# Fewer weight pieces under way beside the feed-forward layers, and half a weight tile requested earlier

## The chip, the cores and the metric

The kernel runs on one core of one Trainium2 chip. A core has a matrix engine (TensorE, PE in the profile), a vector engine (VectorE, DVE), a scalar engine (ScalarE, ACT), a general engine (GpSimd, POOL) and a queue engine (SyncE, SP) that here mainly issues transfers between the chip's memory and the core's own memory. Sixteen DMA engines carry these transfers. The metric is the time of one execution in microseconds (us), as the median of several runs.

## The reference

The program joins two layers. An attention layer with 8 batches, 8 heads, 576 positions and 64 numbers a head (causal in blocks of 64) gives 4608 tokens of 512 numbers. A layer of 8 experts then sends each token to one expert by a gate; an expert keeps at most its 80 best tokens, and every other token's output is zero:

```python
scores = np.where(block_i >= block_j, scale * q @ k.T, -1e9)
attn = softmax(scores);  x = (attn @ v) as (4608, 512)
expert_idx = argmax(x @ w_gate);  gate_w = softmax(x @ w_gate)[expert_idx]
for e in range(8):
    tok_idx = the 80 tokens of expert e with the largest gate_w
    h = np.maximum(x[tok_idx] @ w1[e], 0.0)          # w1[e]: 512 x 1024
    out[tok_idx] = gate_w[tok_idx, None] * (h @ w2[e])  # w2[e]: 1024 x 512
```

All numbers are float32, so an expert's two matrices are 2 MB each and the sixteen of them 32 MB.

## The kernel before, in words

**Attention** takes the first three quarters of the time. It goes over 32 pairs of heads by a table written out by hand, and writes the tokens to a scratch tensor `xs` in the chip's memory (`store_x`, line 391, issued by POOL).

**Selection** follows: the gate's values are ranked, and the numbers of each expert's 80 tokens come out as `gi` (line 1037). POOL then gathers the tokens of the first three experts from `xs` by indirect transfers (`fetch`, line 1027); the first gather needs all writes of `xs` and `gi`.

**The feed-forward layers** start when the first gather has landed. PE turns the tokens (`prepare`, line 1157) and multiplies weights as the stationary operand with 80 tokens as the moving one (`blocks`, line 1144). The order on PE is layer 1 of expert 0, layer 1 of expert 1, layer 2 of expert 0, and so on to layer 2 of expert 7, which is cut in two: three of its four output blocks first, then the last one.

**Weights.** `weights` (line 313) allocates a 2 MB tile and requests it in four pieces (`PARTS`) of 512 KB. The list of 16 tiles (line 309) is in the order of use. The first four go out early through POOL (`early`). The other twelve, 48 pieces, go out through SP's queue at line 327; this text numbers these pieces 1 to 48. Pieces 1 to 8 are two tiles that take memory of the closing attention layer, pieces 9 to 20 three more (`fwa`, `fwc`, `fwb`), and pieces 21 to 48 take the place of tiles that PE has used up; they are asked for in the loop over the experts (lines 1218 and 1224).

SP takes its instructions in order, and what it waits for is set at line 328: a piece waits until the piece three before it (`UNDERWAY`) has landed, so that at most three are under way. Pieces 9 to 20 wait besides for the second gather (`fetches[HOLD]`, line 1124), which the first of them holds back for all behind it. A piece into a used tile waits for PE too.

Of the kernel before, what the change touches and what calls it, by code (L numbers as in the profile page):

```python
# [19 lines left out]
BLK = 64  # L20
NT = 5
FW0, FWA, FWC, FWB = 4, 3, 1, 1
PARTS, UNDERWAY = 4, 3
KPOOL = 2
FIRST, BEHIND = 3, 28
LATER = {(1, 0, 0): 1, (1, 0, 1): 1, (1, 1, 0): 1, (1, 1, 1): 1, (2, 0, 0): 1}
# [129 lines left out]
def tile_attn_moe(ctx, tc, q, k, v, w_gate, w1, w2, capacity, out, xs=None, dbg=None):  # L156
# [3 lines left out]
    E, _, F = w1.shape  # L160
# [88 lines left out]
    before = const.tile([P, P], F32, name="before")  # L249
    after = const.tile([P, P], F32, name="after")  # L250
# [55 lines left out]
    nw = 0  # L306
    wpools = [wp] * FW0

    wlist = [(w1, 0)] + [x for e in range(E) for x in ((w1, e + 1), (w2, e))][0:-2] + [(w2, E - 1)]
    wt_ = {}  # L310
    parts_ = []

    def weights(n, after=None, parts=PARTS, underway=UNDERWAY):

        nonlocal nw
        for _ in range(n):
            src, e = wlist[nw]
            w_ = wpools[nw % len(wpools)].tile([P, KP * F], F32, name="w")
            nw += 1
            wt_[src is w2, e] = w_ = w_.rearrange("p (a f) -> p a f", f=src.shape[2])  # L320
            if nw <= FW0:
                early_.append((w_, src[e].rearrange("(a p) f -> p a f", p=P)))
                continue
            view = src[e].rearrange("(a p) f -> p a f", p=P)
            na = w_.shape[1]
            for a in range(0, na, na // parts):
                load = nc.sync.dma_start(w_[:, a:a + na // parts], view[:, a:a + na // parts]).ins
                for before in ((after,) if after is not None else ()) + tuple(parts_[-underway:][:1] if len(parts_) >= underway else ()):
                    tc.add_manual_dep(load, before.name, mybir.DependencyInfo(
                        mybir.DependencyClass.Sync, mybir.DependencyReason.DATA))  # L330
                parts_.append(load)
# [6 lines left out]
    def early(n):  # L338

        nonlocal begun  # L340
        while n:
            if begun % PARTS == 0:
                weights(1)
            w_, view = early_[-1]
            na = w_.shape[1]
            m = min(n, PARTS - begun % PARTS) if n >= PARTS else 1
            a = slice(na * (begun % PARTS) // PARTS, na * (begun % PARTS + m) // PARTS)
            nc.gpsimd.dma_start(w_[:, a], view[:, a])
            begun += m
            n -= m  # L350
# [462 lines left out]
    n = B * NP  # L813
# [96 lines left out]
    with tc.issue_after(batches[B - 1].stored.ins):  # L910
        pool.indirect_dma_start(
            out=trial, out_offset=None, in_=q.rearrange("b h s d -> (b h s) d"),
            in_offset=bass.IndirectOffsetOnAxis(ap=none.bitcast(U32), axis=0),
            bounds_check=NTOK - 1, oob_is_err=False)
    weights(2)
    sel2 = late.enter_context(tc.tile_pool(name="sel2", bufs=1, **right, **tw))

# [42 lines left out]
    HOLD = 1  # L960
# [65 lines left out]
    def fetch(e, after=None):  # L1026
        load = pool.indirect_dma_start(
            out=xg[e], out_offset=None, in_=xs[:, :],
            in_offset=bass.IndirectOffsetOnAxis(ap=gi[:, e:e + 1].bitcast(U32), axis=0),
            bounds_check=NTOK - 1, oob_is_err=False).ins  # L1030
        if after is not None:
            tc.add_manual_dep(load, after.ins.name, mybir.DependencyInfo(
                mybir.DependencyClass.Sync, mybir.DependencyReason.DATA))
        return load
# [3 lines left out]
    fetches = [fetch(e) for e in range(min(FIRST, E))]  # L1038
# [13 lines left out]
    def finish(after):  # L1052

        with tc.issue_after(after.ins), tc.issue_after(fetches[FIRST - 1]):
            finish_()
# [65 lines left out]
    fwc = late.enter_context(tc.tile_pool(name="fwc", bufs=FWC, **right, **tw))  # L1121
    fwb = late.enter_context(tc.tile_pool(name="fwb", bufs=FWB, **tw))
    wpools += [fwc] * FWC + [fwb] * FWB
    weights(FWA - 2 + FWC + FWB, fetches[HOLD])

    def divide(dst, src, a0=0, a1=NP):

# [38 lines left out]
    def first(e, x_, between=None):  # L1166
        hT = fx.tile([P, FP, CHUNK], F32, name="hT", bufs=3)
        w_ = wt_[False, e]
        for f in range(2):
            ph = ps_s.tile([P, 512], F32, name="ps")  # L1170
            for n_, mm in enumerate(blocks(lambda b: ph[:, b * CHUNK:(b + 1) * CHUNK],
                                           w_[:, :, 512 * f:512 * (f + 1)], x_, KP, 4)):
                if n_ == BEHIND:
                    more(1, e, f, mm)
            nc.scalar.activation(hT[:, 4 * f:4 * (f + 1)].rearrange("p a s -> p (a s)"), ph[:, 0:4 * CHUNK], AF.Relu)  # L1175
            if f == 0 and between is not None:
                between(mm)
        return hT

    def second(e, hT):  # L1180
        py = ps_a.tile([P, 512], F32, name="av")
        for n_, mm in enumerate(blocks(lambda b: py[:, b * CHUNK:(b + 1) * CHUNK], wt_[True, e], hT, FP, KP)):
            if n_ == BEHIND:
                more(2, e, 0, mm)
        yT = fx.tile([P, KP, CHUNK], F32, name="yT", bufs=2)
        vec.tensor_copy(yT.rearrange("p a s -> p (a s)"), py[:, 0:KP * CHUNK])  # L1186
        return yT

    def scatter(e, yT, cuts=(0, KP)):
        y = fx.tile([CHUNK, DM], F32, name="y", bufs=3)  # L1190
        for a0, a1 in zip(cuts, cuts[1:]):
            tp = ps_m.tile([P, 512], F32, name="pm")
            for a in range(a0, a1):
                turned = nc.tensor.transpose(tp[0:CHUNK, a * P:(a + 1) * P], yT[:, a], ident)  # L1194
            vec.tensor_scalar(y[:, a0 * P:a1 * P], tp[0:CHUNK, a0 * P:a1 * P], scalar1=comb[:, 1, e:e + 1], scalar2=None,  # L1195
                              op0=ALU.mult)
            if a1 < KP:
                yield turned
        pool.indirect_dma_start(  # L1199
            out=out[:, :], out_offset=bass.IndirectOffsetOnAxis(ap=si.bitcast(U32)[:, e:e + 1], axis=0),  # L1200
            in_=y, in_offset=None, bounds_check=NTOK - 1, oob_is_err=False)
# [5 lines left out]
    def ready(x, after=None):  # L1207
        xs_[x], divided[x] = prepare(x, after)

    ready(0)  # L1210
    for e in range(E):
        if e + 1 < E and e > 0:
            ready(e + 1)
        if e >= 2:
            for _ in scatter(e - 2, yT_[e - 2]):
                pass
        hT_[e] = first(e, xs_[e], (lambda mm: ready(1, mm)) if e == 0 else None)
        weights(int(nw < len(wlist)))
        if e >= 1:
            yT_[e - 1] = second(e - 1, hT_[e - 1])  # L1220
        if e == 1:
            finish(divided[2])
        if e >= 1:
            weights(int(nw < len(wlist)))
    yl = fx.tile([P, KP, CHUNK], F32, name="yT", bufs=2)
    CUTS = (0, KP - 1, KP)
    tail = scatter(E - 1, yl, CUTS)
# [217 lines left out]
```

## Time and profile before

| what | us |
|---|---|
| median of 3 runs (lowest, highest) | 400.22 (397.24, 400.84) |
| the profiled execution's own time | 396.4 |
| its span, first to last instruction | 394.6 |
| PE busy | 376.5 (95%) |
| DVE busy | 279.9 (71%) |
| ACT busy | 265.1 (67%) |
| POOL busy | 254.7 (65%) |
| TensorE clock granted, of full speed | 0.997 |
| share of PE in the chain that ended last | 82% |

Times in the views count from the first instruction. The profiled execution is one run: the 1.8 us between its span and its time lie before the first and behind the last instruction. The median of the timed runs is 3.8 us above it. A busy PE is not PE at its peak. In the chain of waits, a piece named "issue" is time in which the engine waited for nothing that the profile shows.

### The profile page before, as it was taken

Reading aid. Unit: us, or ns where it says so; the run is one execution under the profiler, and the core shown is the slowest. Engines: PE = TensorE matmul, PEld = TensorE weight load, DVE = VectorE, ACT = ScalarE, POOL = GpSimd, SP = SyncE. Lnnn points to the kernel's source line nnn. Section 1 sums busy time; section 2 is a strip of 40 time slices with the busy share of each in tenths; the row PEclk is TensorE's granted clock in tenths of the full one; section 3 lists DMA queues with packets and bytes.
Section 4 is the critical chain, followed back from the end, with each engine's and each line's share of the span. In section 5 each row is a group of like instructions: output and inputs, shape, how many; then the busy total and the mean of one; then the engine's idle time right before and its main releaser. Section 6 shows DMA issues by size and latency. Waiting matters only on the chain.

```text
span 394.6 us, 15556 instructions
## 1 busy us (share of the span) xinstructions
PE 376.5 (95%) x6351; PEld 292.2 (74%) x6351; DVE 279.9 (71%) x646; ACT 265.1 (67%) x702; POOL 254.7 (65%) x439
## 2 busy tenths in 40 slices
PE   8898999999999999999999999999987989999992
PEld 4576777777777777777777777767765979999892
DVE  5877989998998999899899989988673131111111
ACT  2799898999998999999899989999431111111000
POOL 7889977897798789789979887822567400000011
PEclk9999999999999999999999999999999999999998
DMA  9999999979897898999999999999374999999911
GB/s 139 149 155 152 151 156 197 223 149 226 202 186 167 183 214 201 219 245 257 189 225 271 212 211 240 287 293 312 83 257 132 307 293 321 328 309 305 318 57 39
DMA packets 120125, 84.43 MB, mean 214 GB/s; under 512 B 94446, under 2 KB 96494, under 8 KB 120049
## 3 DMA queue, kind: packets, MB, share of 16 engines
q1 hardware_dynamic: 102432, 45.55, 51.5%
q0 software_dynamic: 15808, 37.52, 40.7%
q8 instruction: 52, 0.85, 1.0%
q10 hardware_dynamic: 1808, 0.31, 0.4%
q14 instruction: 25, 0.20, 0.2%
HBM read 63.22 MB, written 20.33 MB: 212 GB/s over the span
## 4 chain that ended last, share of the span: by engine, by line
PE 82%; POOL 7%; DMA 5%; issue 2%; DVE 2%; POOLq 0%; DVEq 0%
PE sc L650 23%; PE sc L786 20%; PE ps L1144 11%; PE sc L737 11%; PE av L1144 8%; POOL ld L582 2%; PE sc L408 2%; DMA xs<-Y 2%; DMA vn<-in_v_dram 2%; PE sc L745 2%; PE sc L427 1%; PE pm L1194 1%; POOL xs L391 1%; POOL vn L595 1%; PE pm L1157 1%
## 5 line engine op out<-in xcount | busy, mean ns | idle before, releaser
L707 ACT ACTIVATE P<-sc,negm 128x448 f32<-128x448 f32 (+3 forms) x256 | 146.0, 584 | 10.5 <-DVE negm L686 4.1
L686 DVE TENSOR_REDUCE negm<-sc 128x1 f32<-128x448 f32 (+4 forms) x224 | 127.1, 616 | 10.8 <-PE sc L657 9.2
L650 PE MATMUL sc<-T,T 64*128 64x64 f32 (+4 forms) x768 | 111.7, 414 | 2.8 <-POOL T L631 2.1
L650 PEld LDWEIGHTS sc<-T,T 64*128 64x128 f32 x768 | 71.1, 187 | 34.2 <-issue 24.3
L582 POOL DMA_DIRECT2D ld<-in_k_dram x120 | 81.8, 693 | 1.6 <-DMA vn<-in_v_dram 1.0
L798 ACT COPY PT<-sc 128x1024 f32<-128x1024 f32 x63 | 60.8, 1016 | 12.5 <-PE sc L737 11.6
L786 PE MATMUL sc<-PT,vn 128*64 128x128 f32 (+1 forms) x512 | 60.8, 379 | 0.6 <-ACT PT L798 0.6
L737 PE MATMUL sc<-ident,P 64*128 64x64 f32 x1280 | 53.8, 227 | 0.1
L707 ACT ACTIVATION_READ_ACCUMULATOR P<-sc,negm 128x1 f32 x256 | 53.0, 207 | 0.0
L786 PEld LDWEIGHTS sc<-PT,vn 128*64 128x64 f32 x512 | 33.8, 137 | 23.4 <-issue 22.2
L1199 POOL DMA_INDIRECT out_dram<-y,si x8 | 7.4, 924 | 66.7 <-DVE y L1195 60.5
L737 PEld LDWEIGHTS sc<-ident,P 64*128 64x128 f32 x1280 | 45.2, 139 | 3.2 <-ACT P L707 1.2
L628 DVE STREAM_TRANSPOSE T<-ld 128x576 f32<-128x576 f32 x62 | 47.3, 764 | 0.0
L1144 PE MATMUL ps<-xsT,w 128*64 128x80 f32 x1024 | 40.3, 234 | 1.5 <-issue 1.5
L595 POOL DMA_DIRECT2D vn<-in_v_dram x64 | 39.7, 626 | 2.1 <-DMA vn<-in_v_dram 1.6
L1144 PEld LDWEIGHTS ps<-xsT,w 128*64 128x64 f32 x1024 | 37.4, 137 | 3.7 <-issue 2.9
L631 POOL TENSOR_SCALAR T<-T 128x576 f32<-128x576 f32 x31 | 20.7, 668 | 28.6 <-DVE negm L686 13.9
L1186 DVE COPY yT<-av 128x320 f32<-128x320 f32 x7 | 3.4, 492 | 47.5 <-PE av L1144 47.5
L1175 ACT ACTIVATE hT<-ps 128x320 f32<-128x320 f32 x16 | 7.0, 438 | 42.4 <-PE ps L1144 34.4
L1144 PE MATMUL av<-hT,w 128*64 128x80 f32 x896 | 32.9, 233 | 0.7 <-issue 0.7
L1144 PEld LDWEIGHTS av<-hT,w 128*64 128x64 f32 x896 | 32.1, 137 | 0.8 <-issue 0.8
L800 DVE COPY xT<-sc 128x576 f32<-128x576 f32 x31 | 23.3, 752 | 11.5 <-PE sc L764 11.5
(193 smaller groups left out, 526.5 us busy)
## 6 DMA issues: line engine op xcount, KB each, us to landing
w<-in_moe_w_dram SPq DMA_DIRECT2D x48, 512.0 KB
out_dram<-zero SPq DMA_DIRECT2D x18, 512.0 KB
ld<-in_q_dram SPq DMA_DIRECT2D x124, 72.0 KB
ld<-in_k_dram POOLq DMA_DIRECT2D x120, 72.0 KB, 4.9
xs<-Y POOLq DMA_DIRECT2D x28, 288.0 KB, 5.7
vn<-in_v_dram POOLq DMA_DIRECT2D x32, 128.0 KB, 6.3
vn<-in_v_dram POOLq DMA_DIRECT2D x64, 64.0 KB, 5.4
w<-in_moe_w_dram POOLq DMA_DIRECT2D x8, 512.0 KB, 7.0
```

The costliest lines, as they stand in the source:

```text
L582: eng.dma_start(self.nat[x][r], (q, k)[x][self.b, self.h0 + h, :, 32 * i:32 * i + 32] .rearrange("(g r) d -> r g d", r=32))
L595: nc.gpsimd.dma_start(self.vn[c * BLK:(c + 1) * BLK, 1], turned[:, :, 1 - c])
L628: nc.vector.transpose(t, self.nat[x].rearrange("p g d -> p (g d)"))
L631: nc.gpsimd.tensor_scalar(t, t, scalar1=SCALE, scalar2=1.0, op0=ALU.mult, op1=ALU.mult)
L650: nc.tensor.matmul(to[h], lhsT=self.T[0][r, q:q + P], rhs=self.T[1][r, k0:k1], start=start, stop=stop)
L686: nc.vector.tensor_reduce(to, src, axis=AX.X, op=ALU.max, negate=True)
L707: nc.scalar.activation(dst, src, AF.Exp, bias=self.negm[0:n, u, h:h + 1], scale=1.0, accum_out=self.bt.sums[0:n, u, self.h0 + h:self.h0 + ...
L737: nc.tensor.transpose(pt[:, c, to(c, n_)], row[u][r, h, k(u, h, j):k(u, h, j) + P], ident[r, r])
L786: nc.tensor.matmul(to, lhsT=lhs, rhs=rhs, start=(n_ == 0), stop=(n_ == len(steps) - 1))
L798: nc.scalar.copy(*self.out.pop((what, x)))
L800: nc.vector.tensor_copy(*self.out.pop((what, x)))
L1144: yield nc.tensor.matmul(dst(b)[64 * c:64 * (c + 1)], lhsT=w_[:, a, col:col + 64], rhs=x_[:, a], start=(a == 0 and b == 0), stop=(a == n - ...
```

## The change

`weights` gets a parameter `free`: the first `free` pieces of the first tile of a call do not wait for what `after` names. The call for pieces 9 to 20 has `free=2`, so pieces 9 and 10 no longer wait for the second gather. And the calls in the loop over the experts (pieces 21 to 48) use `LATE`, 2, in place of `UNDERWAY`, 3: such a piece waits for the piece two before it.

```diff
-PARTS, UNDERWAY = 4, 3
+PARTS, UNDERWAY, LATE = 4, 3, 2
...
-    def weights(n, after=None, parts=PARTS, underway=UNDERWAY):
+    def weights(n, after=None, parts=PARTS, underway=UNDERWAY, free=0):
...
-        for _ in range(n):
+        for i in range(n):
...
-                for before in ((after,) if after is not None else ()) + tuple(parts_[-underway:][:1] if len(parts_) >= underway else ()):
+                for before in ((after,) if after is not None and (i or a >= free * na // parts) else ()) + tuple(parts_[-underway:][:1] if len(parts_) >= underway else ()):
...
-    weights(FWA - 2 + FWC + FWB, fetches[HOLD])
+    weights(FWA - 2 + FWC + FWB, fetches[HOLD], free=2)
...
-        weights(int(nw < len(wlist)))
+        weights(int(nw < len(wlist)), underway=LATE)
...
-            weights(int(nw < len(wlist)))
+            weights(int(nw < len(wlist)), underway=LATE)
```

The instructions of PE, DVE, ACT and POOL and their order stay as they are; so does the order of SP's transfers. Only waits of SP differ. In the rows below, a transfer waits for counters: `DMAHW0` to `DMAHW7` belong to transfers of SP's queue, which take them in turn, `DMASW0` to `DMASW7` to POOL's in the same way. The gather that is waited for is on `DMASW0`; earlier transfers of POOL are on it too.

SP's queue, pieces 9 to 14 of the change (piece 9 is on `DMAHW3`, so piece 12 waits for it):

```order
L327 DMA w<-in_moe_w_dram 128x2x512 [waits DMASW5_49,DMASW4_49,DMASW6_49,DMASW3_49,DMASW7_49,DMASW1_49,DMAHW0_49,DMASW0_49,Activation_49]
L327 DMA w<-in_moe_w_dram 128x2x512 [waits DMAHW1_49]
L327 DMA w<-in_moe_w_dram 128x2x512 [waits DMAHW2_49,DMASW0_49]
L327 DMA w<-in_moe_w_dram 128x2x512 [waits DMAHW3_49]
L327 DMA w<-in_moe_w_dram 128x1024 [waits DVE_49,PE_49,DMAHW4_49,Activation_49,Pool_49]
L327 DMA w<-in_moe_w_dram 128x1024 [waits DMAHW5_49]
```

The wait for the gather is new on piece 11. Piece 9 waits for `DMASW0` in both kernels, in the change only for the transfers of the attention layer that used its memory.

SP's queue, pieces 21 to 26 before (piece 21 is on `DMAHW7`):

```order
L327 DMA w<-in_moe_w_dram 128x1024 [waits DMAHW4_49,PE_49]
L327 DMA w<-in_moe_w_dram 128x1024 [waits DMAHW5_49]
L327 DMA w<-in_moe_w_dram 128x1024 [waits DMAHW6_49]
L327 DMA w<-in_moe_w_dram 128x1024 [waits DMAHW7_49]
L327 DMA w<-in_moe_w_dram 128x2x512 [waits DMAHW0_49,PE_49]
L327 DMA w<-in_moe_w_dram 128x2x512 [waits DMAHW1_49]
```

The same six pieces in the change:

```order
L327 DMA w<-in_moe_w_dram 128x1024 [waits DMAHW5_49,PE_49]
L327 DMA w<-in_moe_w_dram 128x1024 [waits DMAHW6_49]
L327 DMA w<-in_moe_w_dram 128x1024 [waits DMAHW7_49]
L327 DMA w<-in_moe_w_dram 128x1024 [waits DMAHW0_49]
L327 DMA w<-in_moe_w_dram 128x2x512 [waits DMAHW1_49,PE_49]
L327 DMA w<-in_moe_w_dram 128x2x512 [waits DMAHW4_49,DMAHW2_49]
```

Each waits for the next counter, which is the piece two before it in place of three.

## Rows read from the trace of the kernel before

**Rows 1.** The page: busy tenths in 40 slices of 9.9 us.

```profile
PE   8898999999999999999999999999987989999992
...
DMA  9999999979897898999999999999374999999911
GB/s 139 149 155 152 151 156 197 223 149 226 202 186 167 183 214 201 219 245 257 189 225 271 212 211 240 287 293 312 83 257 132 307 293 321 328 309 305 318 57 39
```

**Rows 2.** Chain of waits, feed-forward layers: start us, us, what.

```profile
322.62 1.24 issue
...
353.96 0.24 issue
...
368.88 0.66 issue
...
381.39 1.26 PE ps L1144 x37
...
383.22 3.05 PE ps L1144 x82
...
388.83 0.64 POOL out_dram L1199
```

**Rows 3.** Timeline of SP's queue: requests of pieces 5, 8, 9, 19-22, 25, 48.

```profile
282.09 0.82 SPq L327 DMA_DIRECT2D w<-in_moe_w_dram  x2
...
286.44 0.33 SPq L327 DMA_DIRECT2D w<-in_moe_w_dram  x1
...
301.82 0.38 SPq L327 DMA_DIRECT2D w<-in_moe_w_dram  x1
...
322.26 0.37 SPq L327 DMA_DIRECT2D w<-in_moe_w_dram  x1
...
324.65 0.37 SPq L327 DMA_DIRECT2D w<-in_moe_w_dram  x1
...
326.02 0.34 SPq L327 DMA_DIRECT2D w<-in_moe_w_dram  x1
...
327.69 0.34 SPq L327 DMA_DIRECT2D w<-in_moe_w_dram  x1
...
331.84 0.38 SPq L327 DMA_DIRECT2D w<-in_moe_w_dram  x1
...
372.09 0.37 SPq L327 DMA_DIRECT2D w<-in_moe_w_dram  x1
```

**Rows 4.** Waits of SP's queue, 255 to 394 us: total us, times, longest.

```profile
SPq L327 <- DMA xg<-xs,gi: 14.8, 1, 14.8
```

**Rows 5.** Waits of SP's queue, 326 to 372 us, all that there are.

```profile
SPq L327 <- DMA w<-in_moe_w_dram: 29.7, 23, 2.1
```

**Rows 6.** Chain of waits from the last writes of `xs` to PE's first turn.

```profile
286.45 7.70 DMA xs<-Y
...
296.06 0.04 POOLq L1027
...
297.23 3.08 DMA xg<-xs,gi
...
300.99 0.36 PE pm L1157 x2
```

**Rows 7.** Busy time by stretch, selection; last columns: clock, DMA share, GB/s.

```profile
289.00:293.00 4.00, 3.85 (x34) 3.00 (x34) 3.44 (x21) 1.41 (x7) 2.28 (x11) 1.00 1.03 365
293.00:296.00 3.00, 2.29 (x24) 1.76 (x26) 2.23 (x9) 1.52 (x8) 2.04 (x4) 1.00 0.18 49
296.00:299.00 3.00, 2.71 (x24) 0.72 (x24) 0.17 (x1) 0.16 (x1) 1.46 (x2) 1.00 0.00 0
```

**Rows 8.** Busy time between PE's three stalls; first columns: PE, weight loads.

```profile
323.86:354.20 30.34, 30.10 (x765) 28.55 (x765) 5.10 (x10) 3.91 (x9) 2.76 (x3) 1.00 0.92 320
354.20:369.54 15.34, 14.68 (x384) 14.05 (x383) 1.24 (x2) 1.74 (x4) 0.92 (x1) 1.00 0.92 309
```

**Rows 9.** The page's DMA queues: packets, MB, share of 16 engines.

```profile
q8 instruction: 52, 0.85, 1.0%
```

## The prediction

> **What bounds the kernel now.** I read the page's slices first. PE is busy at nine tenths or more in nearly every slice; from slice 31 on (306 us) the DMA engines are full too, at 293 to 328 GB/s, and both fall off only at the end [rows 1]. So the change works in a stretch with two nearly full resources, and the question is which has the cushion. The chain of waits answers it: behind 301 us it runs through PE alone, up to the last scatter at 388.83, and its only holes are three of 1.24, 0.24 and 0.66 us in which PE waited for nothing that the profile shows [rows 2]. None of the three is a wait for weights. The weights are ahead of their use, and I ask by how much.
>
> The timeline of SP's queue gives each request. Between 326.02 (piece 21) and 372.09 (piece 48) lie 27 steps, 1.71 us each [rows 3]. In that stretch SP waited for pieces in flight alone, never for PE to free a tile [rows 5]; so the limit on pieces under way sets the rate, and a piece takes 3 x 1.71 = 5.12 us from request to landing on average. Piece 48 then lands near 372.09 + 5.1 = 377.2. It is the last quarter of the last tile, which PE reads by rows of blocks: the first part of that layer has 96 matmul instructions, the last quarter begins at the 73rd, and 37 and 82 of them start at 381.39 and 383.22 [rows 2]: 383.22 + 35 x 3.05/82 = 384.5. The cushion at the end is 384.5 - 377.2 = 7.3 us. Earlier tiles have more.
>
> **Half a tile ahead of the gathers.** Before, SP stood 14.8 us at piece 9 until the second gather had landed [rows 4] and requested it at 301.82 [rows 3]. Now pieces 9 and 10 wait only for pieces 6 and 7, requested between 282.09 and 286.44 [rows 3]. They move 1 MB, 2.9 us at the 365 GB/s of the stretch to 293; after it the engines have 5.5 us of room up to 299 (shares 0.18 and 0.00) [rows 7].
>
> Their cost is at the start. The first gather goes out at 297.23 behind the last writes of `xs` and lands 3.08 us later; PE begins at 300.99 [rows 6], and a delay of these writes delays all behind. Nothing: if the writes were all served by then. At most 2.9 us: if the whole half goes ahead of the last write. From 293 to 296 the engines still had 3 x 0.18 = 0.5 us of transfers [rows 7]; sharing turns with the new pieces these take twice as long. I take **+0.5 us**, near the lower end, since so little was left then. Gathers themselves meet no more than before: pieces 9 and 10 are through, and 11 to 13 go out where 9 to 11 did.
>
> Their gain is a head start. From the second gather on, piece n stands where piece n-2 stood, so piece 21 would be due at piece 19's 322.26. Waiting for one landing more, it goes at piece 20's time, 324.65, and piece 22 at piece 21's, 326.02 [rows 3].
>
> **Two under way in place of three.** Pieces 21 to 48 now make two strands, each requesting its next piece T after the one before, where T is a piece's time from request to landing. Piece 48 is 13 turns behind piece 22 and lands at 326.02 + 14 T; it is in time for 384.5 as long as **T is at most 4.18 us**. The start's 0.5 us moves both and cancels.
>
> No row shows two weight pieces alone on the queue. The lower end is 2/3 of 5.12, 3.41 us: the engines would be the limit, and one piece less in the line would cost no rate. The upper end is 5.12: a piece's time would not fall at all. The nearest rows: 4.15 us is a quick spell with three under way (piece 22 to piece 25), 4.35 us a piece that met a nearly empty weight queue, beside the writes of `xs` (piece 5 to piece 8) [rows 3]. I take their mean, 4.25. Then piece 48 lands at 326.02 + 59.5 = 385.5, 1.0 us late.
>
> There is a page that speaks more kindly of this. The Trainium skill (DMA: Bandwidth & Descriptors, Anatomy of one DMA) fits a transfer as 2.0 us and its bytes at 436 GB/s; by it, as an estimate, 512 KB take 3.2 us and two under way would not be late at all. It is a fit for another issuing path, and both rows above are over 4 us.
>
> **What goes away.** PE's three holes lie 1530 and 767 recorded PE instructions apart, weight loads counted in [rows 8], which is nearly 6 and 3 times 256; the instruction queue moves 0.85 MB in 52 transfers [rows 9], 16 KB each, 256 instructions of 64 bytes. I read the holes as late instruction blocks: the block's transfer stands in line with weight pieces. With one piece less in line the second and third may vanish; the first, at 322.62, falls while three are still under way. Between 0 and 2.1 us, and nothing of it counts if PE waits for weights at the end anyhow. In my forecast: 0. The Trainium skill (Runtime: NRT & Kernel Launch, Instruction fetch mechanics) gives blocks of 16 KB and calls crossing into the next mostly hidden. Seven of the nine crossings here agree, two, and the one at 322.62, do not.
>
> **The sum.** +0.5 at the start, +1.0 for the last piece: the profiled execution's 396.4 would become 397.9. The median is 3.8 us above that execution, and nothing shows where. If in PE's holes, an end set by weights hides it; if elsewhere, it stays. The feed-forward part is 24% of the span (94 of 394.6 us), so I let 0.9 us of the 3.8 be hidden: 397.9 + 2.9 = **400.8 us**, the median before within a microsecond.
>
> **The rivals.**
>
> *The cushion holds and the holes close* (27%). T is at most 4.18, as the quick spell's 4.15 allows. PE keeps the end, and loses up to 2.1 us of holes: 400.2 + 0.5 - 2.1 = 398.6. If much of the 3.8 us of the median is of the same kind, down to 395. Against it: of the nine blocks of [rows 8] seven were crossed without a hole, and the largest hole is outside the new limit. The Trainium skill's fit (DMA: Bandwidth & Descriptors, Anatomy of one DMA) points this way.
>
> *The feed-forward layers become bound by latency* (15%). A piece spends its time in fixed parts and not in the line; T stays near 4.6. Piece 48 lands at 390.4, 5.9 us late, the waits for pieces 41 to 48 come one after another on PE, and with the start it is 406.6. At 5.12 it would be 397.7, 13.2 us late: 413.9. It is slower by over 1% from T = 4.43 on (326.02 + 14 x 4.43 = 388.0, 3.5 late, plus 0.5). For it: DMA engines at 293 to 328 GB/s were below the 365 of the earlier stretch, so they were not saturated throughout [rows 1, 7]. Against it: 4.15 and 4.35 were seen.
>
> *The early half holds the writes of `xs` or the first gather back* (6%), 2.9 us: 403.1, decided by which queue the engines serve.
>
> That the change does nothing is excluded: the wait counters of all 28 pieces have moved, and SP had no other wait there [rows 5].
>
> **How the numbers follow.** Forecast 52%: T between 4.18 and about 4.4, 399 to 404. Its middle is 400.8. Range 396.8 to 406.0: it takes in most of the first rival, leaving out its lower tail, and the milder half of the second. One per cent, 4.0 us, is about what a measurement of this kernel can tell from no change. Faster by more: 7%, all from the first rival, which needs most of the 3.8 us as well. Slower by more: 18%, 15 from the second rival, 3 from the edges of the others. Within: 75%.
>
> **What would show it.** In the timeline of SP's queue: piece 9 requested ahead of 296; from piece 21 on steps of T/2 = 2.1 us in place of 1.71, and the last request near 381 in place of 372. In the slices: DMA below nine tenths, and about 250 GB/s, from slice 33 to 38. In the chain: holes of about a microsecond on PE at quarters of the last tile. The first gather's request half a microsecond later. I am wrong if PE has no hole in the last 15 us and the early ones are gone (the cushion held), if holes start well before the last tile's first use at 381 us (latency), or if PE's first turn moves by over 1.5 us.

## The result and the profile after

The change made the kernel slower: 402.68 us (median of 4 runs, 400.96 to 405.61) against 399.05 (4 runs, 397.24 to 400.84). The ratio is 1.0113, with an interval from 1.0069 to 1.0158; the two medians alone are 0.9% apart. A ratio in this text leaves out executions more than 1.5% above the fastest of their kernel, so a kernel whose times spread widely has its median beside the ratio. The profiled execution took 400.96 us with a span of 399.2, 4.6 us more than the profiled one of before.

The page of the changed kernel, busy tenths in 40 slices of 10 us:

```profile
PE   8899999999999999999999999999878999999962
...
PEclk9999999999999999999999999999998999999997
DMA  9999999969889999999999998995777987877870
GB/s 141 147 157 154 151 177 188 214 149 230 204 163 178 226 191 211 217 269 222 227 241 249 192 239 204 329 297 179 217 239 239 296 256 233 253 221 240 251 247 24
```

Against [rows 1] the DMA engines are no longer full beside the feed-forward layers: 221 to 256 GB/s from slice 32 on, where it had been 293 to 328, and they are still at 247 in slice 38, where it had been 57 and the last weights landed early in the slice. PE's digits hide the end of the story; a slice of 10 us with 3 us of waits shows little.

SP's queue, the requests of pieces 5, 9, 10, 21, 22 and 48:

```profile
281.54 0.82 SPq L327 DMA_DIRECT2D w<-in_moe_w_dram  x2
...
288.82 0.38 SPq L327 DMA_DIRECT2D w<-in_moe_w_dram  x1
...
291.77 0.38 SPq L327 DMA_DIRECT2D w<-in_moe_w_dram  x1
...
322.84 0.34 SPq L327 DMA_DIRECT2D w<-in_moe_w_dram  x1
...
325.29 0.34 SPq L327 DMA_DIRECT2D w<-in_moe_w_dram  x1
...
384.62 0.37 SPq L327 DMA_DIRECT2D w<-in_moe_w_dram  x1
```

Pieces 9 and 10 went out ahead of the gathers, as meant, and pieces 21 and 22 3.2 and 2.4 us earlier than in [rows 3]. But from piece 22 to piece 48 a strand made 13 turns in 59.33 us, **4.56 us a turn** on average, 2.28 us a piece in place of 1.71. The last request came at 384.62 in place of 372.09.

PE's timeline at the end of the same kernel (start, length, what, how many; in brackets the idle time before and what ended it):

```profile
375.95 2.42 PE L1144 MATMUL av<-hT,w 128*64 128x80 f32 x63
378.94 1.33 PE L1144 MATMUL av<-hT,w 128*64 128x80 f32 x32 [0.57 <-DMA w<-in_moe_w_dram]
380.45 1.33 PE L1144 MATMUL av<-hT,w 128*64 128x80 f32 x32 [0.19 <-DMA w<-in_moe_w_dram]
383.00 1.05 PE L1144 MATMUL ps<-hT,w 128*64 128x80 f32 x24 [1.22 <-DMA w<-in_moe_w_dram]
384.64 0.77 PE L1144 MATMUL ps<-hT,w 128*64 128x80 f32 x14 [0.59 <-DMA w<-in_moe_w_dram]
...
387.11 1.05 PE L1144 MATMUL ps<-hT,w 128*64 128x80 f32 x24 [0.57 <-SPq L1254]
388.88 1.88 PE L1144 MATMUL ps<-hT,w 128*64 128x80 f32 x48 [0.72 <-SPq L1254]
```

The idle times stand at counts of 32 and 24 instructions, which are quarters of the last two tiles: PE takes a piece, is done with it and waits for the next. The waits for pieces 43 to 48 are 0.57 + 0.19 + 1.22 + 0.59 + 0.57 + 0.72 = 3.9 us. The releaser of the last two is named wrongly (an event of SP that was merely the latest); piece 48, requested at 384.62, lands about 4.3 us later, when PE goes on at 388.88. From there to the end of the span it is 10.3 us, much as before (10.1 us from 384.5).

The start: POOL's first gather and PE's first turn of the changed kernel, one row of each engine's timeline:

```profile
296.65 1.08 POOL L1027 DMA_INDIRECT xg<-xs,gi  x1 [2.14 <-DVE gi L1037]
```

```profile
300.46 0.80 PE L1157 MATMUL pm<-ident,xn 80*128 80x80 f32 x4 [2.27 <-DVE xn L1132]
```

In this execution everything from the end of the attention on was half a microsecond earlier. A delay of the writes of `xs` would show ahead of the gather's issue: from the request of piece 5 to that issue it is 15.11 us here and 15.14 before [rows 3, 6], and POOL's row names `gi`, not a write, as what released the gather. A delay of the gather itself would show behind the issue: to PE's turn 3.81 us went by, 3.76 before [rows 6]. The early half cost the start nothing in this execution.

### The profile page after: what moved, and what is told of

Its sections match the earlier page's. It is cut to its first block, busy times and chain, and to the rows that moved or that the text cites. A ratio compares the mean times of both kernels' runs of the same rounds, so it can differ in the third digit from the quotient of the medians.

```text
span 399.2 us, 15558 instructions
## 1 busy us (share of the span) xinstructions
PE 378.4 (95%) x6351; PEld 293.6 (74%) x6351; DVE 280.1 (70%) x646; ACT 265.1 (66%) x702; POOL 254.4 (64%) x439
## 5 line engine op out<-in xcount | busy, mean ns | idle before, releaser
L1144 PE MATMUL ps<-xsT,w 128*64 128x80 f32 x1024 | 41.4, 239 | 0.1
L1144 PEld LDWEIGHTS ps<-xsT,w 128*64 128x64 f32 x1024 | 38.6, 140 | 2.2 <-issue 1.4
```

The lines of the kernel that those rows point to most:

```text
L1144: yield nc.tensor.matmul(dst(b)[64 * c:64 * (c + 1)], lhsT=w_[:, a, col:col + 64], rhs=x_[:, a], start=(a == 0 and b == 0), stop=(a == n - ...
```

## The experiments

All ratios are against runs of the kernel before on the same chip in the same session.

### Each part alone

```diff
early_only
-PARTS, UNDERWAY, LATE = 4, 3, 2
+PARTS, UNDERWAY, LATE = 4, 3, 3
two_only
-    weights(FWA - 2 + FWC + FWB, fetches[HOLD], free=2)
+    weights(FWA - 2 + FWC + FWB, fetches[HOLD], free=0)
```

early_only: 

> Only the early half tile: pieces 9 and 10 free of the second gather, three under way throughout. Theory (the turn of two late pieces sets the tail): no wait of PE for weights in the tail, last piece requested near 369 (3 us ahead of the 372.09 of before), first gather not later; time as before, 398 to 400, ratio 0.997 to 1.003. Rival (the early half is what costs, through the writes of xs, the gathers or the fuller DMA engines): 401 to 403 as the change.

two_only: 

> Only two pieces under way from piece 21 on; pieces 9 to 20 all wait for the second gather as before. Theory: the same turns of 4.5 us, begun 3 us later, so the last piece is requested near 388 and PE's tail waits grow by about 3 us against the change: 405 to 407. Rival (the early half is what costs): 399 to 400.

`two_only` took 406.89 us, ratio 1.0203 (1.0175 to 1.0231). SP's queue in it, pieces 21, 22 and 48:

```profile
328.11 0.34 SPq L327 DMA_DIRECT2D w<-in_moe_w_dram  x1
329.36 0.70 SPq L327 DMA_DIRECT2D w<-in_moe_w_dram  x1
...
390.26 0.37 SPq L327 DMA_DIRECT2D w<-in_moe_w_dram  x1
```

Thirteen turns in 60.9 us, 4.68 each, begun 4 to 5 us later than in the change, and the last request 5.6 us later. The early half is worth about 4 us of time when two are under way (406.89 against 402.68, which are of two sessions; by their ratios 3.6 us): the rule of two is the cost, and the early half repays part of it.

`early_only` had a ratio of 0.9956 (0.9912 to 1.0000), which rests on 5 of its 12 executions; the median of all is 400.39 against 398.77, and they range from 394.36 to 402.62. Its last piece went out at 369.10 and PE had no wait for weights, as expected; alone it is neither a clear gain nor a clear loss. Two things that can spread its times, PE's holes and the granted clock, come below.

### More and less of each

```diff
whole_tile
-    weights(FWA - 2 + FWC + FWB, fetches[HOLD], free=2)
+    weights(FWA - 2 + FWC + FWB, fetches[HOLD], free=4)
taper (both calls in the loop)
-        weights(int(nw < len(wlist)), underway=LATE)
+        weights(int(nw < len(wlist)), underway=LATE if nw < 12 else UNDERWAY)
```

whole_tile: 

> Two under way as in the change, but the whole tile (pieces 9 to 12) free of the second gather. Theory: the chain of pieces is two further ahead, last request 3 to 4 us earlier (near 381), PE's waits for weights nearly gone: 398.5 to 400.5. Rival (early pieces delay the gathers): pieces 11 and 12 meet the first gathers, PE starts over half a microsecond later than in the change, 403 to 405.

taper: 

> Early half as in the change; two under way only for pieces 21 to 32, three again for 33 to 48. Theory: 12 pieces at 2.3 us and 16 at 1.7 us end near 378 with the last request, the last piece lands near 383 and is in time: PE without waits for weights, 398 to 400. Rival (two under way costs by another way than late pieces at the end): 401 to 403.

`whole_tile` took 399.88, ratio 1.0041 (1.0016 to 1.0065). The theory's time held, and of the rival its delay but not its 403 to 405. The last request came at 381.28 (3.3 us earlier than in the change) and PE had no wait for weights. And the gathers did meet pieces 11 and 12, requested at 294.87 and 296.81: from the first gather's issue to PE's first turn it is 5.51 us in place of 3.81, and that turn comes 2.4 us later than the change's, after twice the idle time. The rows of POOL and PE:

```profile
297.37 1.08 POOL L1027 DMA_INDIRECT xg<-xs,gi  x1 [2.66 <-issue]
...
302.88 1.09 PE L1157 MATMUL pm<-ident,xn 80*128 80x80 f32 x4 [4.49 <-DVE xn L1132]
```

So the half tile fits ahead of the gathers and the next megabyte does not. In this kernel the head start was still worth more than the delay: it is quicker than the change.

`taper` took 399.63 against 398.77, ratio 0.9985 (0.9946 to 1.0025, from 8 of its 12 executions): with two under way for 12 pieces only, the last request is at 378.17, PE has no wait for weights, and the slowdown of the change is gone. Two under way costs by the late pieces at the end; any other cost is below what these runs can tell.

### A piece's time by the number under way

```diff
one_under
-PARTS, UNDERWAY, LATE = 4, 3, 2
+PARTS, UNDERWAY, LATE = 4, 3, 1
four_under
+PARTS, UNDERWAY, LATE = 4, 3, 4
```

one_under: 

> One piece under way from piece 21 on, to measure a piece's time from request to landing without any other weight piece ahead of it. Theory (most of a piece's time is fixed and not spent in the line): about 4.1 us a piece, not much under the 4.56 us with two under way, so steps of 4.1 us, 28 of them, PE starved, near 450 us. Rival (time is spent in the line): half of 4.56, 2.3 us a piece, then steps as in the change and about 403 us.

four_under: 

> Four pieces under way from piece 21 on, early half as in the change. Theory: with four the engines are the limit, steps of 1.5 to 1.65 us and a piece takes over 6 us; weights are far ahead, and PE's holes at the ends of 256-instruction blocks are at least those of three under way (2 to 5 us in a profile) and more than with two (0.5 us): 399 to 403. Rival (the holes have nothing to do with the weight pieces in the line): holes as with two under way, 396 to 398.

SP's queue, pieces 22 and 48 of `one_under`:

```profile
330.32 0.34 SPq L327 DMA_DIRECT2D w<-in_moe_w_dram  x1
...
432.23 0.37 SPq L327 DMA_DIRECT2D w<-in_moe_w_dram  x1
```

The same two of `four_under`:

```profile
321.41 0.34 SPq L327 DMA_DIRECT2D w<-in_moe_w_dram  x1
...
361.12 0.37 SPq L327 DMA_DIRECT2D w<-in_moe_w_dram  x1
```

| under way | us a piece takes to its turn | us between pieces | from |
|---|---|---|---|
| 1 | 3.92 | 3.92 | `one_under`, 26 steps in 101.91 us |
| 2 | 4.56 to 4.68 | 2.28 to 2.34 | the change, `two_only`, `whole_tile` (13 turns in 60.22) |
| 3 | 5.12 to 5.26 | 1.71 to 1.75 | before [rows 3], `early_only` (27 steps in 47.30 us) |
| 4 | 6.11 | 1.53 | `four_under`, 26 steps in 39.71 us |

These are means; single steps of `one_under` run from 3.4 to 5.4 us, turns of the change from 3.7 to 5.9. A piece with no other weight piece under way takes 3.92 us, and each further one adds 0.6 to 0.9 us. So with two under way most of a piece's time is its own and not spent behind the other. `one_under` took 452.39 us (one execution), as the theory had it. `four_under` had a median of 401.98 and a ratio of 1.0078 (1.0037 to 1.0119); nine executions lie between 399.50 and 406.57, and one took 613.78 us at a mean clock of 0.624. Weights were far ahead, and it was slower than three under way all the same.

### The holes in PE

A likely reason is in PE's timeline. In `four_under`, with no weight late, its idle times behind 314 us ended by nothing shown are

```profile
314.69 4.70 PE L1144 MATMUL av<-hT,w 128*64 128x80 f32 x126 [1.10 <-issue]
...
320.89 0.56 PE L1071 MATMUL ps<-RG,OH 128*80 128x32 bf16 x10 [1.32 <-issue]
...
333.49 1.73 PE L1144 MATMUL av<-hT,w 128*64 128x80 f32 x21 [2.29 <-issue]
...
345.63 1.32 PE L1144 MATMUL av<-hT,w 128*64 128x80 f32 x30 [0.42 <-issue]
...
366.45 1.74 PE L1144 MATMUL av<-hT,w 128*64 128x80 f32 x44 [0.35 <-issue]
```

and in the profiled execution of `early_only`, with three under way (401.2 us, one of its longer ones),

```profile
319.82 0.56 PE L1071 MATMUL ps<-RG,OH 128*80 128x32 bf16 x10 [1.57 <-issue]
...
332.12 0.97 PE L1144 MATMUL av<-hT,w 128*64 128x80 f32 x21 [1.92 <-issue]
...
353.31 1.60 PE L1144 MATMUL av<-hT,w 128*64 128x80 f32 x39 [0.85 <-issue]
...
374.27 0.91 PE L1144 MATMUL av<-hT,w 128*64 128x80 f32 x20 [0.83 <-issue]
```

Busy time of `early_only` between those holes (first columns: PE and weight loads, with counts):

```profile
319.83:332.13 12.30, 10.38 (x257) 9.72 (x257) 3.35 (x18) 1.48 (x4) 0.97 (x1) 1.00 0.91 290
332.13:353.31 21.18, 20.33 (x511) 19.13 (x512) 3.86 (x8) 2.60 (x6) 1.84 (x2) 1.00 0.90 302
353.31:374.28 20.97, 20.14 (x512) 19.06 (x512) 2.48 (x4) 2.60 (x6) 1.83 (x2) 1.00 0.91 302
```

They are 514, 1023 and 1024 instructions apart, within two of 2, 4 and 4 times 256; these counts take in instructions at both edges and leave out PE's semaphore instructions. Counted one by one in the traces with these, the holes of `early_only` lie 512, 1024 and 1024 instructions apart and those of `four_under` 256, 512, 512 and 1024. The hole at 332.12 of `early_only`, that at 333.49 of `four_under` and one at 327.91 of `taper_warm`, a kernel of a later section, stand behind the same number of instructions from the program's start, though `taper_warm` has 32 more ahead of the feed-forward layers. So the holes go by instruction count and not by what is computed there, and the reading of [rows 8, 9] as late instruction blocks holds in other kernels; no view shows the block's own transfer arriving late. Their cost can be more than their length: behind the hole of 2.29 us in `four_under` the granted clock was at 0.50, the lower of its two levels (1.2 and 2.4 GHz), for 2 us.

From 326 to 375 us, beside the feed-forward pieces, they sum to 0.9 us before (the two later ones of [rows 2]), 3.6 in `early_only`, 3.1 in `four_under` and 0.8 in `before_warm`, a kernel of a later section: three or four under way. With two under way there was none in that stretch in the change, `whole_tile`, `taper`, and `change_warm` and `no_last_tile` below, and none in `two_only` from its piece 21 at 328.11 until weights were late. Two cases speak against a simple rule: `whole_tile` had one of 0.82 us at 321.4, and `taper_warm` the one of 1.32 that began at 326.59, both a few microseconds into their stretch with two. And `taper`, back at three under way from 352 us on, had none from there to 375 either; its one late hole, of 1.70 us, lies behind the stretch summed here:

```profile
381.34 1.88 PE L1144 MATMUL av<-hT,w 128*64 128x80 f32 x48 [1.70 <-issue]
```

That fewer pieces in line shorten the holes is borne out by most of the profiles, and not settled: a profile is one execution, and the holes of one kernel vary.

### Is the end set by the weights?

```diff
change_warm
-WARM = [10, 11, 6, 8, 3]
+WARM = [10, 11, 6, 8, 5]
no_last_tile
-    wlist = [(w1, 0)] + [...][0:-2] + [(w2, E - 1)]
+    wlist = [(w1, 0)] + [...][0:-2]
...
+    wt_[True, E - 1] = wt_[True, E - 2]
```

change_warm: 

> The change with the two more turns of idle matmuls. Theory (landing weights set its end, not PE): the clock stays up at the start, but PE only waits longer for the last pieces: 402 to 403.5, as the change, last request near 384.5 still. Rival (PE's speed sets the end): 2 us faster, 400 to 401, as the turns gave the kernel before.

no_last_tile: 

> The change without the load of the last weight tile (pieces 45 to 48): expert 7's second layer reads expert 6's weights, so the output differs there. Theory: the waits of 3.1 us for pieces 45 to 48 go, those for pieces 41 to 44 stay (0.8 us): 398.5 to 400. Rival (the waits are not what makes the end late): 402 to 403, as the change.

`no_last_tile`, which leaves out the load of the last weight tile and reads the tile before it in its place, took 398.51, ratio 1.0014 (0.9974 to 1.0054), as expected. Its profiled execution was its longest, 401.17 us, and had longer waits for pieces 42 to 44 (3.0 us in place of the 0.8 expected), but PE's timeline shows the point: behind them nothing waits.

```profile
380.86 1.33 PE L1144 MATMUL av<-hT,w 128*64 128x80 f32 x32 [1.90 <-DMA w<-in_moe_w_dram]
382.56 1.33 PE L1144 MATMUL av<-hT,w 128*64 128x80 f32 x32 [0.38 <-SPq L1255]
384.58 1.33 PE L1144 MATMUL av<-hT,w 128*64 128x80 f32 x32 [0.69 <-SPq L1255]
385.74 1.55 PE L1144 MATMUL ps<-hT,w 128*64 128x80 f32 x38
```

`change_warm`, with a faster PE at the start (next section), took 401.21 against 399.33, ratio 1.0103 (1.0004 to 1.0202). Its times don't decide: 401.21 lies between the theory's 402 to 403.5 and the rival's 400 to 401, and the interval of the ratio holds both. The profile does. The last request was at 384.11, 0.5 us earlier than in the change; PE waited longer for single pieces, up to 2.01 us, and went on with piece 48 at 388.54, where the change had 388.88:

```profile
380.43 1.33 PE L1144 MATMUL av<-hT,w 128*64 128x80 f32 x32 [2.01 <-DMA w<-in_moe_w_dram]
...
388.54 1.88 PE L1144 MATMUL ps<-hT,w 128*64 128x80 f32 x48 [1.07 <-SPq L1254]
```

The landing of the last pieces sets the changed kernel's end: a faster PE waits for them, and without the last four the slowdown is gone.

### The idle matmuls ahead of the feed-forward layers

```diff
taper_warm (on taper), before_warm (on the kernel before)
-WARM = [10, 11, 6, 8, 3]
+WARM = [10, 11, 6, 8, 5]
```

taper_warm: 

> The kernel with two under way for pieces 21 to 32 alone, and two more turns of the idle matmuls (WARM[4] 5 in place of 3) that end near 300.4 us, so that PE stands still for half a microsecond in place of 2.5 ahead of the feed-forward layers. Theory: the granted clock stays at full speed there (it fell to 0.5 to 0.8 from 301 to 307 us in five of the six profiles), worth about 2 us in the executions that lost it: 396 to 397.5, clocks of 0.994 and over in all. Rival (the clock falls for another reason, or the start is delayed by the extra matmuls): 399 to 401, clocks as before.

before_warm: 

> The kernel before with the same two more turns of idle matmuls and nothing else. Theory: clocks of 0.994 and over in all executions, 396 to 397.5, and where PE has holes they stand at other matmuls but still whole multiples of 256 instructions apart. Rival: 398 to 400, as before.

`WARM[4]` is the number of turns of matmuls without a use that PE runs ahead of the feed-forward layers (line 1040 of the changed kernel). Busy time of the change from PE's start on (last columns: granted clock, DMA share, GB/s):

```profile
301.00:304.00 3.00, 3.00 (x54) 2.91 (x56) 2.36 (x11) 0.44 (x2) 2.67 (x8) 0.66 0.51 141
304.00:307.00 3.00, 3.00 (x60) 2.74 (x59) 0.04 (x1) 0.86 (x2) 1.03 (x1) 0.77 1.05 408
307.00:310.00 3.00, 3.00 (x80) 2.82 (x78) 0.00 (x0) 0.84 (x2) 0.97 (x1) 1.00 0.95 253
```

The same of `before_warm`:

```profile
301.00:304.00 3.00, 2.88 (x68) 2.62 (x68) 2.20 (x7) 0.58 (x2) 2.68 (x9) 1.00 0.59 121
304.00:307.00 3.00, 3.00 (x76) 2.73 (x72) 0.57 (x8) 0.84 (x2) 1.44 (x3) 1.00 1.05 391
```

The change's profile ran part of its first six microseconds there at the lower of the clock's two levels, 1.2 GHz (a mean of 0.5 would be all of it), and issued 54 + 60 matmuls where `before_warm` has 68 + 76. PE had stood still for 2.27 us before. The profile of before had stood as long (2.28 us) and kept 1.00. With two more turns of idle matmuls PE stood still for 0.79 us in `before_warm` and 0.74 in `taper_warm`, and the clock stayed up: over 12 executions each, the mean clock of `taper_warm` was 0.995 to 0.997 and of `before_warm` 0.993 to 0.997 (0.994 was expected as the least), where 29 executions of the kernel before in that session had 0.985 to 0.997. Of these 29, the 8 at 0.993 or more have a median of 396.6 us, the other 21 of 399.5. Medians of the two kernels: 397.14 and 396.89 against 398.99. The ratios are 0.9972 each (0.9942 to 1.0001, 0.9938 to 1.0006). `before_warm` has the lowest median of all kernels tried, below both the kernel before and the change; its interval, as that of `taper_warm`, just touches no difference.

## Why the prediction was right or wrong, point by point

- **What bounds the kernel: right.** PE's chain with weights 7 us ahead was the right thing to weigh. Take the cushion away and waits appear at the quarters of the last tile, where they were looked for, but also at the last two quarters of the tile before it: the first begins at 378.4. Waits that start before the last tile's use were the sign named for the latency rival, and in this it came true.
- **The early half, +0.5 us at the start: wrong, it was nothing** (15.11 us from piece 5 to the gather against 15.14, and 3.81 from there to PE against 3.76). The writes of `xs` were not held back. `whole_tile` shows a late start, but by the second megabyte and on the gather itself: 2.4 us.
- **The head start: right.** Piece 22 was due at 326.02 + 0.5 and went at 325.29. Of these 1.2 us, 0.5 is the start that cost nothing and another 0.5 that this execution ran earlier.
- **T, the mis-sized term.** I took 4.25 us, a mean of two rows; it measured 4.56. Over 13 turns that is 4.0 us on the last request; less the 1.2 us by which piece 22 went earlier, the forecast's 1.5 us becomes 4.3, and the profile's was 4.6. One of the two rows, 4.15, was the quickest of many spells with three under way, and a quick spell of a noisy line is no measure of a shorter line. One row nearer to the mean of 5.12 would have been better: the table says 0.6 us less per piece taken out. The break-even, T = 4.18, fits the waits that came, but no run had a T near it.
- **The rival bound by latency.** Its T of 4.6 is what happened, and it had 15%. Its price of 406.6 was 3.9 us too high. On the profile that is 1.8 us (6.4 priced, 4.6 measured): the start cost nothing (0.5), piece 22 went 0.7 us earlier than priced, and T was 4.56, not 4.6 (0.5 over 14 turns). The rest is the distance of the median from the profile, 3.8 us in the price and 1.7 in the changed kernel.
- **The rival that the cushion holds: fell,** but its second half was right. The holes closed, to 0.51 us in the change's profile behind 301; as the forecast said, nothing of that counts while PE waits for weights. Two under way can't be all of the reason: the longest hole of before, at 322.62, was missing too, though three were still under way there.
- **The Trainium skill's fit** (DMA: Bandwidth & Descriptors, Anatomy of one DMA): by it, as an estimate, 512 KB take 3.2 us. A lone piece took 3.92 here on SP's path, so the measurement decides. All pieces had 512 KB, so no run shows how the time goes with the bytes.
- **The sum.** 400.8 us was forecast, with a range of 396.8 to 406.0, and most chance on within 1%. The time was 402.68 and the change 1.1% slower, at the edge of what that bound can tell (interval 0.7 to 1.6%). The direction of the sum was right and its size too small by T. That it came so near is in part luck: the profiled execution was forecast at 397.9 and took 400.96, 3.1 us more, while the 2.9 us added from there to the median turned out to be 1.7. And T = 4.56 lies outside the forecast's own branch of 4.18 to 4.4.

## What to carry to other kernels

The number of transfers under way is a trade between rate and whoever else stands in the line; before lowering it, take the cushion of the last transfer and divide it by the number of turns, and compare that with a measured turn, because a turn shrinks by much less than its share when one transfer is taken out. A limit can be low where the cushion is large and must be high where the cushion is used up, as `taper` did without the change's loss. And when executions of one kernel spread over 2%, look at the granted clock of each before crediting an edit.

## What the runs showed of the hardware

- A 512 KB weight piece took 3.92 us from its request to the request that waited for it when no other weight piece was under way, 4.6 with one other, 5.2 with two and 6.1 with three others; the rate rose by 1.7, 1.3 and 1.1 times per step.
- Idle times of PE with no releaser in the profile, read here as late instruction blocks, came to 5.5 us in one execution (the five holes of `four_under` above), whole multiples of 256 instructions apart where they were counted.
- Two executions of nearly the same idle stretch (2.3 us of PE at rest) came out with the clock kept at 1.00 in one and at a mean of 0.66 and 0.77 for the next six microseconds in the other. In `two_only` it fell again behind the 2.34 us wait at the end, where 32 matmuls took 2.40 us in place of 1.33:

```profile
382.75 1.33 PE L1144 MATMUL av<-hT,w 128*64 128x80 f32 x32 [0.38 <-DMA w<-in_moe_w_dram]
386.42 2.40 PE L1144 MATMUL av<-hT,w 128*64 128x80 f32 x32 [2.34 <-DMA w<-in_moe_w_dram]
```

The clock also fell, to 0.50, behind the hole of 2.29 us in `four_under`, and a little over a microsecond behind the 2.01 us wait of `change_warm`; it stayed at 1.00 behind waits and holes of 1.90 us (`no_last_tile`), 1.92 (`early_only`) and the 2.28 of the kernel before. What decides whether an idle stretch of this length loses the clock stays open; the idle stretches of 0.74, 0.79 and 0.92 us in the three kernels with more idle matmuls kept it.
